# Where the first weight tiles of a fused retention and two-MLP kernel are loaded and converted

## The chip, the cores and the metric

The kernel runs on one core of a Trainium2 chip. The metric is device time in microseconds (us) for one launch. Times are medians of several runs; the profile is of one execution.

## The reference

Three layers follow one another, in float32. The first is linear attention with a decay per head ("retention") for 2 sequences of 768 positions, 8 heads of 64. Its output, 1536 tokens of 512 values, goes through a softplus MLP (512 to 2048 to 512) and then through an RMS-normalized SwiGLU MLP (512 to 1536 to 512).

```
state = gamma * state + k[t] outer v[t]          # per head, t = 0 .. 767
y[t]  = scale * q[t] @ state
x = y as (1536, 512)
x = softplus(x @ w_in) @ w_out
n = x / sqrt(mean(x * x) + 1e-6) * rms_g
out = (silu(n @ w_gate) * (n @ w_val)) @ w_out2
```

The weights of the MLPs arrive as 64-bit floats.

## The kernel before

**Tiles.** Tokens are handled in 12 chunks of 128 (6 for each sequence) and 4 blocks of 384 tokens (3 chunks each; `CB` is 3, `NB` is 4). A weight matrix is cut into tiles of 512 KB of doubles, 16 of `w_in` and 16 of `w_out`, used in groups of four: four of `w_in`, then four of `w_out`. Products are made in three terms of high and low parts, so that each value stands as two `fp32r` tiles.

**A chunk.** `load_next` starts the DMAs of q and k of one chunk and v of the chunk before it. `prep` scales v on POOL (GpSimd). `step_t` transposes k and q on PE (TensorE); ACT (ScalarE) copies k, DVE (VectorE) multiplies q by a table. `step_s` makes the scores on PE, and DVE multiplies them by two masks. `step_y` makes y on PE; ACT takes the high part of it and DVE the low part (`split`), and that is the x of the first MLP. `step_u` updates the state.

**A weight tile.** `load_weight` issues its DMA into one of three staging buffers (`STAGE`), if fewer than three tiles are loaded and not yet converted. `convert` turns the doubles into two float32 parts, in three pieces. The first is queued at once: two ACT reads of the staged tile (`c`, L166, and `a`, L167), two DVE operations (`w`, L168 and L170) and an add on POOL (L172). The second (`finish`: one DVE multiply, L181) and the third (`last`: the high part on ACT, L123, the low part on POOL, L124) are put on a list. `flush` runs what is on that list at that moment, and, if its argument is not false, calls `load_weight` as well. `weight` is what a product calls for its tile; where the tile isn't finished, it converts and flushes until it is:

```
while order[i] not in ready:
    if pos["conv"] <= i:
        assert convert()
    flush()
```

**The order of the work.** Everything is written out by hand: each engine works through its own queue in the order of the program. All loads but two stand on the queue of SP. An instruction that waits, a DMA issue too, holds what stands behind it on its queue. PSUM has eight banks that are taken in turn.

The front is the loop over `g` at L551. It takes chunks 0 to 2 to their x and prepares chunks 3 and 4. Behind it is the loop over weight groups `gr` and blocks `b`. In the first group the block that is multiplied is one ahead of the chunks still to be made: in each of four iterations `o`, `step_t` of a later chunk, the product `l1` of this block with one `w_in` tile (12 matmuls), then `step_y`, `step_u`, `step_s` of a chunk, and in block 0 one `convert` at the end. `l1`'s result goes through Abs, Exp and Ln on ACT (L358 to L360), a DVE operation (L361), and a split. In block 1, from the third iteration on, `l2` multiplies block 0's result by all four `w_out` tiles (12 matmuls for each of four outputs).

Of the kernel before, what the change touches and what calls it, by code (L numbers as in the profile page):

```python
# [27 lines left out]
def retention_softplus_swiglu(ctx: ExitStack, tc: tile.TileContext, q, k, v, w_in, w_out,  # L28
# [10 lines left out]
    CB = T // P  # L39
# [61 lines left out]
    def load_next(g, weight=False):  # L101
        if g + 1 < NCH:
            load(g + 1, 0)
            load(g + 1, 1)
        if weight:
            load_weight()
        if g < NCH:
            load(g, 2)
# [32 lines left out]
    def load_weight():  # L141
        i = pos["load"]
        if i >= len(order) or i >= pos["conv"] + STAGE:
            return False
        nm, f = order[i]
        t = stage_p.tile([P, N, 2], U32, tag="stage", name=f"st_{nm}{f}")
        src = srcs[nm]
        if nm in ("w_out", "w_out2"):
            nc.sync.dma_start(out=t, in_=src[f * P:(f + 1) * P])
        else:  # L150
            nc.sync.dma_start(out=t.rearrange("p (k f) two -> p k f two", k=KC),
                              in_=src[:, f * P:(f + 1) * P].rearrange("(k p) f two -> p k f two", p=P))
        staged[i] = t
        pos["load"] += 1
        return True

    def convert():
        i = pos["conv"]
        if i >= pos["load"] or not free:
            return False  # L160
        st = staged.pop(i)
        lo32, hi32 = st[:, :, 0], st[:, :, 1]
        c = cv_p.tile([P, N], U32, tag="c", name="c")
        a = cv_p.tile([P, N], F32, tag="a", name="a", bufs=3)
        w = cv_p.tile([P, N], U32, tag="w", name="w")
        nc.scalar.activation(out=c, in_=lo32, func=AF.Copy, scale=2.0 ** -29)  # L166
        nc.scalar.activation(out=a, in_=hi32.bitcast(F32), func=AF.Abs)  # L167
        nc.vector.tensor_scalar(out=w, in0=hi32, scalar1=3, scalar2=0x3FFFFFF8,  # L168
                                op0=ALU.logical_shift_left, op1=ALU.bitwise_and)
        nc.vector.scalar_tensor_tensor(out=w, in0=hi32, scalar=0xC0000000, in1=w,  # L170
                                       op0=ALU.bitwise_and, op1=ALU.bitwise_or)
        nc.gpsimd.tensor_tensor(out=c, in0=w, in1=c, op=ALU.add)  # L172
        slot[order[i]] = free.pop(0)
        t = ws_p.tile([P, 2, N], F32R, tag=f"ws{slot[order[i]]}", name=f"ws_{order[i][0]}")

        def last():
            split(t[:, 0], t[:, 1], a, nc.gpsimd)
            ready.add(order[i])

        def finish():  # L180
            nc.vector.scalar_tensor_tensor(out=a, in0=a, scalar=TINY, in1=c.bitcast(F32),  # L181
                                           op0=ALU.is_ge, op1=ALU.mult)
            deferred.append(last)


        deferred.append(finish if order[i][0] in ("w_in", "w_out") else lambda: deferred.append(finish))
        ws[order[i]] = t
        left[order[i]] = NB
        pos["conv"] += 1
        return True  # L190
# [12 lines left out]
    def flush(loads=True):  # L203
        todo = list(deferred)
        deferred.clear()
        for s in todo:
            s()
        if loads:
            load_weight()
# [39 lines left out]
    def prep(g):  # L249
        t = qkv[g][2]  # L250
        nc.gpsimd.tensor_tensor(out=t, in0=t, in1=dec[:, 1, 0, :, None].to_broadcast([P, H, D]), op=ALU.mult)
# [19 lines left out]
    def step_t(g, busy=0, order=(1, 0)):  # L271
        turn(g, busy, order)
        turned(g, order)

    def step_s(g):
        t = tr[g]
        sc = [bank("sc").rearrange("p (j t) -> p j t", j=NP) for _ in range(2)]
        for j in range(NP):
            for e in range(2):
                r = slice(e * D, (e + 1) * D)  # L280
                nc.tensor.matmul(sc[e][:, j, :], lhsT=t[r, 1, j, :], rhs=t[r, 0, j, :], start=True, stop=True)
        for e in range(2):
            nc.vector.tensor_tensor(out=t[:, 2 + e], in0=sc[e], in1=mask[e], op=ALU.mult)

    def step_u(g):
        c = g % CPB
        _, kk, vv = [qkv[g].pop(i) for i in range(3)]
        if c == CPB - 1:
            return
        u = bank("u")[:, 0:NP * D].rearrange("p (j t) -> p j t", j=NP)  # L290
        for j in range(NP):
            for e in range(2):
                h = 2 * j + e
                nc.tensor.matmul(u[e * D:(e + 1) * D, j, :], lhsT=kk[:, h, :], rhs=vv[:, NP * e + j, :],
                                 start=True, stop=True, skip_group_check=True)
        new, old = state[(c + 1) % 2], state[c % 2]
        if c == 0:
            nc.vector.tensor_copy(new, u)
        else:
            for j in range(NP):  # L300
                nc.vector.scalar_tensor_tensor(out=new[:, j], in0=old[:, j], scalar=step[:, j:j + 1], in1=u[:, j],
                                               op0=ALU.mult, op1=ALU.add)

    def step_y(g):
        c = g % CPB
        bi, ci = divmod(g, CB)
        if ci == 0:
            x[bi] = x_p.tile([P, 2, KC, T], F32R, tag="x", name=f"x{bi}")


        ys = [bank("y")[:, 0:2 * P].rearrange("p (i t) -> p i t", i=2) for _ in range(2)]
        t = tr.pop(g)

        if c:
            for i in range(2):
                for e, h in ((0, 0), (1, 1), (0, 1), (1, 0)):
                    nc.tensor.matmul(ys[e][h * D:(h + 1) * D, i, :], lhsT=state[c % 2][e * D:(e + 1) * D, 2 * i + h, :],
                                     rhs=t[e * D:(e + 1) * D, 0, 2 * i + h, :], start=(i == 0), stop=False,
                                     skip_group_check=True)
        for e in range(2):  # L320
            for i in range(2):
                for h in range(2):
                    j = 2 * i + h
                    nc.tensor.matmul(ys[e][h * D:(h + 1) * D, i, :], lhsT=qkv[g][2][:, NP * e + j, :], rhs=t[:, 2 + e, j, :],
                                     start=(c == 0 and i == 0), stop=True, skip_group_check=True)
        sl = slice(ci * P, (ci + 1) * P)
        for e in range(2):
            k2 = slice(2 * e, 2 * e + 2)
            split(x[bi][:, 0, k2, sl], x[bi][:, 1, k2, sl], ys[e])
# [220 lines left out]
    nc.scalar.activation(out=step, in_=tab[:, 0, :, 0], func=AF.Copy, scale=float(D) ** 0.5)  # L550
    for g in range(CB):  # L551
        load_next(g + 2)
        if g:
            load_weight()
        prep(g + 1)
        if g == CB - 1:
            nc.sync.dma_start(out=rg, in_=rms_g.rearrange("(k p) -> p k", p=P))
        step_y(g)
        step_u(g)
        step_s(g + 1)  # L560
        flush(False)
        if g < CB - 1:
            step_t(g + 2)
        flush(False)
        if 0 < g < CB - 1:
            convert()

    pend = None
    for gr in range(NG1):
        for b in range(NB):  # L570
# [6 lines left out]
            if gr == 0 and b < NB - 1:  # L577
                for o in range(G1):
                    g = (b + 1) * CB + o
# [95 lines left out]
```

## Time and profile before

| What | us |
|---|---|
| Median of 3 runs (lowest, highest) | 697.7 (696.85, 698.48) |
| The profiled execution | 698.23 |
| Its span in the profile | 696.5 |
| PE busy | 644.7 |
| DVE busy | 415.0 |
| ACT busy | 339.5 |
| POOL busy | 197.1 |

The span is from the first to the last instruction that the profiler saw; some 1.7 us of the execution lie around it. Busy shares are means over stages that differ: the first 140 us hold the attention and the first products, the rest is a dense succession of matmuls. L-numbers are lines of the kernel. "DMA share" is the mean busy share of 16 DMA engines.

### The profile page before, as it was taken

Reading aid. Unit: us, or ns where it says so; the run is one execution under the profiler, and the core shown is the slowest. Engines: PE = TensorE matmul, PEld = TensorE weight load, DVE = VectorE, ACT = ScalarE, POOL = GpSimd, SP = SyncE. Lnnn points to the kernel's source line nnn. Section 1 sums busy time; section 2 is a strip of 40 time slices with the busy share of each in tenths; the row PEclk is TensorE's granted clock in tenths of the full one; section 3 lists DMA queues with packets and bytes.
Section 4 is the critical chain, followed back from the end, with each engine's and each line's share of the span. In section 5 each row is a group of like instructions: output and inputs, shape, how many; then the busy total and the mean of one; then the engine's idle time right before and its main releaser. Section 6 shows DMA issues by size and latency. Waiting matters only on the chain.

```text
span 696.5 us, 10150 instructions
## 1 busy us (share of the span) xinstructions
PE 644.7 (93%) x3980; PEld 610.8 (88%) x3980; DVE 415.0 (60%) x713; ACT 339.5 (49%) x656; POOL 197.1 (28%) x156
## 2 busy tenths in 40 slices
PE   8656779999999999999999869999999999999997
PEld 7545668899999999999899759999999999999996
DVE  5643743545657574847657985586548773783432
ACT  3432723578767676759567543554225332441111
POOL 1322440336323241414101441263205330440000
PEclk9977979999999999999999989999999999999999
DMA  9945630223212120203001330132002220200112
GB/s 199 228 111 118 147 82 1 62 68 115 67 54 76 47 91 31 91 31 97 25 1 51 100 93 1 60 122 62 31 30 96 63 84 2 91 1 15 46 46 75
DMA packets 65567, 48.93 MB, mean 70 GB/s; under 512 B 39792, under 2 KB 60528, under 8 KB 65520
## 3 DMA queue, kind: packets, MB, share of 16 engines
q1 hardware_dynamic: 64320, 47.90, 24.5%
q8 instruction: 31, 0.51, 0.3%
q10 hardware_dynamic: 1200, 0.39, 0.2%
q14 instruction: 16, 0.13, 0.1%
HBM read 45.14 MB, written 3.15 MB: 69 GB/s over the span
## 4 chain that ended last, share of the span: by engine, by line
PE 60%; DVE 17%; ACT 13%; POOL 4%; issue 3%; SPq 2%; DMA 1%; POOLq 0%
PE h_w_val L341 12%; PE h_w_gate L341 11%; PE h L341 10%; PE l L495 9%; PE l L377 5%; PE acc L495 5%; PE acc L341 3%; POOL c L172 3%; DVE a L181 3%; DVE t L361 2%; ACT t L359 2%; PE acc L377 2%; ACT t L360 2%; DVE g L124 2%; DVE w L170 2%
## 5 line engine op out<-in xcount | busy, mean ns | idle before, releaser
L172 POOL TENSOR_TENSOR c<-w,c 128x512 uint32<-128x512 uint32 x68 | 89.0, 1308 | 335.1 <-DVE w L170 237.7
L341 PE MATMUL h<-x,ws_w_in 128*128 128x384 f32 x756 | 147.0, 343 | 13.4 <-ACT ws_w_in L123 13.0
L341 PEld LDWEIGHTS h<-x,ws_w_in 128*128 128x128 f32 x756 | 136.2, 194 | 14.4 <-ACT ws_w_in L123 13.7
L123 ACT ACTIVATE g<-t 128x384 fp32r<-128x384 f32 x112 | 58.7, 524 | 122.4 <-DVE t L476 84.2
L361 DVE SCALAR_TENSOR_TENSOR t<-h,t 128x384 f32<-128x384 f32 x63 | 35.1, 558 | 114.4 <-ACT t L360 114.4
L377 PE MATMUL l<-g,ws_w_out 128*128 128x384 f32 x516 | 97.4, 336 | 2.9 <-DVE g L124 1.4
L124 DVE TENSOR_TENSOR g<-t,g 128x384 fp32r<-128x384 f32 x112 | 75.2, 671 | 36.3 <-ACT g L123 35.3
L341 PE MATMUL h_w_val<-xn,ws_w_val 128*128 128x384 f32 x504 | 94.9, 336 | 0.0
L377 PEld LDWEIGHTS l<-g,ws_w_out 128*128 128x128 f32 x516 | 89.7, 188 | 4.5 <-DVE g L124 2.5
L341 PE MATMUL h_w_gate<-xn,ws_w_gate 128*128 128x384 f32 x492 | 92.7, 336 | 0.0
L341 PEld LDWEIGHTS h_w_val<-xn,ws_w_val 128*128 128x128 f32 x504 | 88.9, 188 | 2.3
L341 PEld LDWEIGHTS h_w_gate<-xn,ws_w_gate 128*128 128x128 f32 x492 | 87.0, 189 | 1.1
L495 PE MATMUL l<-ws_w_out,g 128*128 128x512 f32 x288 | 72.8, 396 | 3.8 <-ACT ws_w_out L123 2.8
L472 ACT ACTIVATE t<-t 128x384 f32<-128x384 f32 x48 | 25.2, 525 | 97.4 <-DVE t L471 97.4
L181 DVE SCALAR_TENSOR_TENSOR a<-a,c 128x512 f32<-128x512 f32 x68 | 62.7, 921 | 15.3 <-POOL c L172 15.2
L495 PEld LDWEIGHTS l<-ws_w_out,g 128*128 128x128 f32 x288 | 53.5, 188 | 14.4 <-ACT ws_w_out L123 3.3
L377 PE MATMUL acc<-g,ws_w_out 128*128 128x384 f32 x252 | 50.2, 348 | 5.0 <-ACT ws_w_out L123 4.2
L358 ACT ACTIVATE t<-h 128x384 f32<-128x384 f32 x63 | 30.4, 483 | 44.5 <-PE h L341 44.5
L476 DVE TENSOR_TENSOR t<-h_w_val,t 128x384 f32<-128x384 f32 x42 | 23.3, 554 | 47.6 <-PE h_w_val L341 46.4
L377 PEld LDWEIGHTS acc<-g,ws_w_out 128*128 128x128 f32 x252 | 45.8, 196 | 6.2 <-ACT ws_w_out L123 4.4
L124 POOL TENSOR_TENSOR ws_w_out<-a,ws_w_out 128x512 fp32r<-128x512 f32 x28 | 39.3, 1402 | 36.5 <-ACT ws_w_out L123 32.4
L495 PE MATMUL acc<-ws_w_out,g 128*128 128x512 f32 x144 | 35.4, 392 | 0.0
(122 smaller groups left out, 813.7 us busy)
## 6 DMA issues: line engine op xcount, KB each, us to landing
st_w_out<-in_moe_w_out_dram SPq DMA_DIRECT2D x28, 512.0 KB, 3.4
st_w_in<-in_moe_w_in_dram SPq DMA_DIRECT2D x16, 512.0 KB, 3.8
st_w_gate<-in_moe_w_gate_dram SPq DMA_DIRECT2D x12, 512.0 KB, 3.7
st_w_val<-in_moe_w_val_dram SPq DMA_DIRECT2D x12, 512.0 KB, 3.6
v<-in_v_dram SPq DMA_DIRECT2D x12, 256.0 KB, 4.6
q<-in_q_dram SPq DMA_DIRECT2D x23, 128.0 KB, 4.0
k<-in_k_dram SPq DMA_DIRECT2D x23, 128.0 KB, 4.0
out_dram<-o SPq DMA_DIRECT2D x11, 256.0 KB, 2.0
```

The source lines that it names most:

```text
L123: nc.scalar.activation(out=hi, in_=src, func=AF.Copy)
L124: eng.tensor_tensor(out=lo, in0=src, in1=hi.bitcast(F32), op=ALU.subtract)
L170: nc.vector.scalar_tensor_tensor(out=w, in0=hi32, scalar=0xC0000000, in1=w, op0=ALU.bitwise_and, op1=ALU.bitwise_or)
L172: nc.gpsimd.tensor_tensor(out=c, in0=w, in1=c, op=ALU.add)
L181: nc.vector.scalar_tensor_tensor(out=a, in0=a, scalar=TINY, in1=c.bitcast(F32), op0=ALU.is_ge, op1=ALU.mult)
L341: nc.tensor.matmul(h, lhsT=w[:, i, kk * P:(kk + 1) * P], rhs=src[:, j, kk, :], start=(n == 0), stop=(n == 3 * KC - 1))
L358: nc.scalar.activation(out=t, in_=h, func=AF.Abs)
L361: nc.vector.scalar_tensor_tensor(out=t, in0=h, scalar=0.0, in1=t, op0=ALU.max, op1=ALU.add)
L377: nc.tensor.matmul(p, lhsT=w[:, i, m * P:(m + 1) * P], rhs=g_t[b, f][:, j, :], start=(n == 0 and f == (0 if keep else fs[0])), stop=(n == ...
L472: nc.scalar.activation(out=t, in_=t, func=AF.Silu)
L476: nc.vector.tensor_tensor(out=t, in0=h, in1=t, op=ALU.mult)
L495: nc.tensor.matmul(p, lhsT=g_t[b, f][:, j, m * P:(m + 1) * P], rhs=w[:, i, :], start=(n == 0 and f == (0 if keep else grp[0])), stop=(n == ...
```

## The change

The front loads a weight tile with each of its three chunks, where it did so with the second and third only, and converts one tile in each of its three passes, where it did so in the second only. The rest of the code is the same; since conversions are counted, all later ones up to the fourth block stand elsewhere too.

```
     for g in range(CB):
         load_next(g + 2)
-        if g:
-            load_weight()
+        load_weight()
         prep(g + 1)
...
         flush(False)
         if g < CB - 1:
             step_t(g + 2)
         flush(False)
-        if 0 < g < CB - 1:
+        if True:
             convert()
```

On SP, in the front, from v of chunk 2 on; `st_` are weight tiles, and the names' numbers count allocations. Before:

```order
L81 DMA v_210<-in_v_dram 128x8x64
L84 DMA q_263<-in_q_dram 128x4x64 x2
L84 DMA k_266<-in_k_dram 128x4x64 x2
L81 DMA v_269<-in_v_dram 128x8x64
L151 DMA st_w_in_271<-in_moe_w_in_dram 128x4x256
L84 DMA q_343<-in_q_dram 128x4x64 x2
L84 DMA k_346<-in_k_dram 128x4x64 x2
L81 DMA v_349<-in_v_dram 128x8x64
L151 DMA st_w_in_351<-in_moe_w_in_dram 128x4x256
```

And now, the same stretch:

```order
L81 DMA v_210<-in_v_dram 128x8x64
L151 DMA st_w_in_212<-in_moe_w_in_dram 128x4x256
L84 DMA q_274<-in_q_dram 128x4x64 x2
L84 DMA k_277<-in_k_dram 128x4x64 x2
L81 DMA v_280<-in_v_dram 128x8x64
L151 DMA st_w_in_282<-in_moe_w_in_dram 128x4x256
L84 DMA q_357<-in_q_dram 128x4x64 x2
L84 DMA k_360<-in_k_dram 128x4x64 x2
L81 DMA v_363<-in_v_dram 128x8x64
L151 DMA st_w_in_365<-in_moe_w_in_dram 128x4x256
```

Every weight tile from the second on stands one chunk (q, k, v) further ahead.

On ACT, in the front, from the copy of chunk 2's k on; `x_` rows are the splits of a chunk's y, `c` and `a` the two reads of a staged weight tile, `ws_w_in` its high part. Before:

```order
L269 ACTIVATE at<-pt 128x512
L123 ACTIVATE x_213<-y 128x2x128
L123 ACTIVATE x_213<-acc_275 128x2x128
L269 ACTIVATE at<-acc_322 128x512
L166 ACTIVATE c<-st_w_in_172 128x512
L167 ACTIVATE a<-st_w_in_172 128x512
L123 ACTIVATE x_213<-acc_355 128x2x128
L123 ACTIVATE x_213<-y 128x2x128
L123 ACTIVATE ws_w_in<-a 128x512
L269 ACTIVATE at<-pt 128x512
L358 ACTIVATE t<-h 128x384
```

And now, up to the same split of chunk 2 and one row more:

```order
L269 ACTIVATE at<-pt 128x512
L166 ACTIVATE c<-st_w_in_172 128x512
L167 ACTIVATE a<-st_w_in_172 128x512
L123 ACTIVATE x_215<-y 128x2x128
L123 ACTIVATE x_215<-acc_286 128x2x128
L269 ACTIVATE at<-acc_334 128x512
L123 ACTIVATE ws_w_in<-a 128x512
L166 ACTIVATE c<-st_w_in_212 128x512
L167 ACTIVATE a<-st_w_in_212 128x512
L123 ACTIVATE x_215<-acc_369 128x2x128
L123 ACTIVATE x_215<-y 128x2x128
L123 ACTIVATE ws_w_in<-a 128x512
```

The first tile is read ahead of the split of chunk 1, the second ahead of that of chunk 2; behind these rows the third is read ahead of the first softplus (L358).

On DVE, in the third iteration of block 1, from a split to the next softplus; `w` are the rows of a conversion, here the tile that `l2` demands. Before:

```order
L124 TENSOR_TENSOR x_783<-acc_982,x_783 128x2x128
L301 SCALAR_TENSOR_TENSOR state_120<-state_119,step,u 128x64 x4
L283 TENSOR_TENSOR at<-sc,mask 128x512
L283 TENSOR_TENSOR at<-acc_1017,mask 128x512
L168 TENSOR_SCALAR w<-st_w_out_781 128x512
L170 SCALAR_TENSOR_TENSOR w<-st_w_out_781,w 128x512
L181 SCALAR_TENSOR_TENSOR a<-a,c 128x512
L361 SCALAR_TENSOR_TENSOR t<-h,t 128x384
```

And now:

```order
L124 TENSOR_TENSOR x_811<-acc_1010,x_811 128x2x128
L301 SCALAR_TENSOR_TENSOR state_120<-state_119,step,u 128x64 x4
L283 TENSOR_TENSOR at<-sc,mask 128x512
L283 TENSOR_TENSOR at<-acc_1045,mask 128x512
L361 SCALAR_TENSOR_TENSOR t<-h,t 128x384
```

The conversion of the fourth `w_out` tile is gone from here; it now stands in the first iteration of this block.

## Rows read from the trace of the kernel before

**Rows 1.** The page: busy tenths in 40 slices of 17.4 us, and PE's granted clock.

```profile
PE   8656779999999999999999869999999999999997
...
PEclk9977979999999999999999989999999999999999
```

**Rows 2.** Waits of PE over the span: us in total, times, longest.

```profile
PE h L341 <- ACT ws_w_in L123: 13.0, 3, 5.7
PE acc L341 <- ACT ws_w_in L123: 6.0, 1, 6.0
PE acc L377 <- ACT ws_w_out L123: 4.2, 1, 4.2
PE acc L262 <- DVE at L283: 3.6, 1, 3.6
```

**Rows 3.** Timeline of PE, first loop: start, duration, what [idle before, releaser].

```profile
25.50 2.38 PE L341 MATMUL h<-x,ws_w_in 128*128 128x384 f32 x12 [1.61 <-ACT ws_w_in L123]
...
31.48 0.60 PE L262 MATMUL acc<-ident,q 128*128 128x128 f32 x4
37.80 4.21 PE L341 MATMUL h<-x,ws_w_in 128*128 128x384 f32 x12 [5.71 <-ACT ws_w_in L123]
...
65.74 4.01 PE L341 MATMUL acc<-x,ws_w_in 128*128 128x384 f32 x12 [6.00 <-ACT ws_w_in L123]
69.59 2.27 PE L341 MATMUL h<-x,ws_w_in 128*128 128x384 f32 x12
```

**Rows 4.** Timeline of PE, the first products with `w_out`.

```profile
94.17 1.68 PE L377 MATMUL acc<-g,ws_w_out 128*128 128x384 f32 x8
...
100.97 1.01 PE L377 MATMUL acc<-g,ws_w_out 128*128 128x384 f32 x2 [4.19 <-ACT ws_w_out L123]
...
108.87 4.32 PE L377 MATMUL acc<-g,ws_w_out 128*128 128x384 f32 x24
```

**Rows 5.** Two windows: length, engines' busy us, then PEclk, DMA share, GB/s.

```profile
0.00:17.40 17.40, 14.87 (x176) 13.17 (x176) 9.86 (x22) 5.30 (x10) 3.22 (x10) 1.00 1.02 199
17.40:34.80 17.40, 11.92 (x164) 10.27 (x164) 11.18 (x27) 7.86 (x16) 5.68 (x5) 1.00 0.98 228
```

**Rows 6.** Timeline of SP's queue: when weight tiles one and three are issued.

```profile
8.95 1.11 SPq L151 DMA_DIRECT2D st_w_in<-in_moe_w_in_dram  x1
...
24.84 1.05 SPq L151 DMA_DIRECT2D st_w_in<-in_moe_w_in_dram  x1
```

**Rows 7.** DMA issues, 8.9 to 9.5 and 24.8 to 25.0: size, us to landing.

```profile
st_w_in<-in_moe_w_in_dram SPq DMA_DIRECT2D x1, 512.0 KB, 5.5
...
st_w_in<-in_moe_w_in_dram SPq DMA_DIRECT2D x1, 512.0 KB, 5.6
```

**Rows 8.** Timeline of POOL: the scaling of chunk 2's v.

```profile
19.12 1.04 POOL L251 TENSOR_TENSOR v<-v,dec 128x512 f32<-128x512 f32 x1 [5.43 <-DMA v<-in_v_dram]
```

**Rows 9.** Timeline of ACT in the front.

```profile
13.24 0.60 ACT L269 ACTIVATE at<-pt 128x512 f32<-128x512 f32 x1 [1.80 <-PE pt L262]
14.82 0.38 ACT L123 ACTIVATE x<-y 128x256 fp32r<-128x256 f32 x1 [0.98 <-PE y L324]
...
19.40 0.67 ACT L166 ACTIVATE c<-st_w_in 128x512 uint32<-128x512 uint32 x1
...
20.92 0.39 ACT L123 ACTIVATE x<-acc 128x256 fp32r<-128x256 f32 x1 [0.27 <-PE acc L324]
...
27.92 0.49 ACT L358 ACTIVATE t<-h 128x384 f32<-128x384 f32 x1 [1.99 <-PE h L341]
```

**Rows 10.** Timeline of DVE: a loop iteration's first and last, and conversion multiplies.

```profile
29.55 0.56 DVE L361 SCALAR_TENSOR_TENSOR t<-h,t 128x384 f32<-128x384 f32 x1 [4.17 <-ACT t L360]
...
34.87 0.68 DVE L264 TENSOR_TENSOR at<-acc,tab 128x512 f32<-128x512 f32 x1
36.39 0.69 DVE L181 SCALAR_TENSOR_TENSOR a<-a,c 128x512 f32<-128x512 f32 x1 [0.84 <-POOL c L172]
...
75.70 1.47 DVE L181 SCALAR_TENSOR_TENSOR a<-a,c 128x512 f32<-128x512 f32 x1
```

More of the change, by code (lines that the diff above doesn't have):

```diff
@@ L552, in retention_softplus_swiglu @@
         load_next(g + 2)
-        if g:
-            load_weight()
+        load_weight()
         prep(g + 1)
@@ L564, in retention_softplus_swiglu @@
         flush(False)
-        if 0 < g < CB - 1:
+        if True:
             convert()
```

## The prediction

> **What bounds the kernel now.** I read the slices first. PE (TensorE) is busy nine tenths or more of nearly every slice from about 105 us on; in front of that it is busy five to eight tenths, and the granted clock sags there too [rows 1]. So a change in the front pays in full if PE reaches its dense part earlier.
>
> Then the waits of PE: four stalls on ScalarE's weight tile `ws_w_in` (13.0 us in three, 6.0 us in one), one of 4.2 us on `ws_w_out`, and one of 3.6 us of transposes behind DVE's masks [rows 2]. PE's timeline places them. The first projection of the loop starts at 25.50, the second at 37.80 after 5.71 us idle, the fourth at 65.74 after 6.00 [rows 3]; the third waits much the same, for 13.0 less 5.7 leaves it up to 5.7. The code says why: one `convert()` stands at the end of each iteration, and the next `l1` demands that tile, so the whole chain of seven operations over ACT, DVE and POOL lies between two projections. The idle time costs clock as well: twelve matmuls take 2.38 us at 25.50 (2.4 GHz), 4.21 and 4.01 us after such a stall (1.2 GHz) [rows 3]. Later, two pieces of `l2` and a projection of 2.3 us lie between 94.17 and 108.87, with the 4.19 us stall among them: 14.7 - 2.3 = 12.4 us for a pair of `l2`; the pair at 108.87 takes 4.32 [rows 4].
>
> **The change, part by part.** The order of the instructions shows that it does what it says: three conversions stand in the front instead of one, the weight loads stand one chunk earlier on SP, and the conversion that `l2` demands in the second block is gone. No instruction is added or removed.
>
> *Transfers.* In the front the queue is saturated: 0.98 of the engines at 228 GB/s between 17.4 and 34.8 us [rows 5]. A weight tile of 0.524 MB is then worth 2.3 us, a chunk's q, k and v (0.786 MB) 3.45 us. The order is unchanged up to v of chunk 2, which is on the chip at 19.1 [rows 8]. Counting on from there in the new order, estimated landings are: second weight tile 21.4, q and k of chunk 4 23.7, v of chunk 3 24.8, third tile 27.1, q and k of chunk 5 29.4, v of chunk 4 30.6, fourth tile 32.9, q and k of chunk 6 35.2, v of chunk 5 36.3, two w_out tiles 38.6 and 40.9, q and k of chunk 7 43.2. A check: before, the third tile was issued at 24.84 and took 5.6 us [rows 6, 7], so 30.4; it now stands ahead of one chunk (3.45), which gives 27.0. SP waits for a free staging buffer from the fourth tile on, and the conversions that free them now come early.
>
> *Front, g = 0.* The first tile lands at 8.95 + 5.5 = 14.45 [rows 6, 7]. ACT comes to it after the copy at 13.24, waits 0.6 us and reads it twice, some 1.3 us (0.67 each [rows 9]). The split of chunk 1 behind it then begins at 15.8 instead of 14.82 [rows 9], 1 us late. I cost that at nothing: the y of chunk 2, next on PE, needs its scaled v, which POOL starts at 19.12 [rows 8]. Without that cover it would be 1 us.
>
> *g = 1.* ACT is ready for the second tile before it lands at 21.4, and reads it until 22.7; the split of chunk 2 behind it began at 20.92 [rows 9], so it is 1.8 us late, and DVE's work after it as much. PE is not held by that: the first `l1` has its weight, and starts when chunk 4 has been transposed, 23.7 + 1.1 = 24.8, against 25.50 [rows 3]. It ends at 27.1.
>
> *g = 2.* The third tile holds ACT until 27.1 + 1.3 = 28.4, the copy of k until 29.0; the first softplus takes 1.63 us from ACT's start to DVE's (27.92 to 29.55 [rows 9, 10]), so DVE begins at 30.6, 1.05 us later than now. That is the loss of the change.
>
> *Loop.* PE's own work for one iteration is 6.6 us (25.50 to 31.48 + 0.60 [rows 3]). DVE's train, from its first operation at 29.55 to the end of the last, 34.87 + 0.68, is 6.0 us; less 0.6 idle in it, plus the 0.69 of the conversion's multiply [rows 10], 6.1. When the multiply met work of POOL it took 1.47 instead of 0.69 [rows 10]: 6.9. I take 6.9 for an iteration; the bounds are PE's 6.6 and, if three DVE operations were held like this in each, 6.1 + 3 x 0.78 = 8.4. The transfers need 2.3 + 3.45 = 5.75 us, under all of these. Step by step: DVE starts at 30.6; its masks end 4.4 us later (6.1 less 1.7 for the three operations behind them), at 35.0, and the y of chunk 4 can go; that of chunk 5 goes one iteration later, 41.9. From there it is one round of PE, 6.6 us, to the first `l1` of the second block: 48.5. (In that round the transposes of chunk 7 are due at about 44.7; their data land at 43.2.) Before, that `l1` started at 69.59 [rows 3]: **21.1 us**.
>
> *Second block.* Its iterations stay as they are, the 3.6 us stall among them. At `l2` the last w_out tile has been converted an iteration earlier, so the 12.4 us become the 4.3 of the pair without a wait [rows 4]: **8.1 us**. The lower bound is 4.2, if the stall alone goes and the low clock stays.
>
> *Later.* From the fourth pass of the first weight group on the loads stand in the same order as before; nothing is gained or paid.
>
> **Sum.** 21.1 + 8.1 = 29.2 us, off a profiled execution of 698.2 (span 696.5), which lies 0.5 above the median of 697.7. So 697.7 - 29.2 = **668.5 us**.
>
> One rule speaks against this. The multiply at 75.70 took 1.47 us, with POOL at work beside it, and 0.69 at 36.39 [rows 10]. The Trainium skill, "SBUF — State Buffer", section "Who interferes with whom", says that a DVE instruction with both inputs in SBUF and a GpSimd instruction that reads SBUF want one port, which is an exclusive lock: the second waits until the first is done. By that rule the conversions, which so far ran while the rest stood still, would now hold DVE's operations of the loop more often. The trace agrees for the multiply; for the other two-input operations no row here shows it.
>
> **Rivals.**
> - *Transfers late.* For: the front's share of 0.98 [rows 5]. Against: in the loop 5.75 us of transfers meet 6.9 of work. At the 199 GB/s of the first stretch [rows 5] the 5.5 MB from 19.1 to chunk 7's data end at 46.7, not 43.2; its transposes wait 2 us, the conversions that hold ACT another 2: 672.5, and 676 if a pause of the queue comes on top. Chance 0.15.
> - *POOL and DVE hold one another*, as a mechanism of this kernel: 8.4 instead of 6.9 us in three iterations, and the same once in block two, 1.5 x 4 = 6: 674.5. For: the 1.47; against: other operations of the same train keep their length. Chance 0.15.
> - *The stall on w_out stays*, or a new one takes its place: 668.5 + 8.1 = 676.6. Against: its conversion stands an iteration earlier in the order. Chance 0.05.
> - *More is gained*: the 3.6 us stall of block two goes as well [rows 2]: 664.9, or 664 with the clock behind it. Chance 0.09.
> - *The change doesn't do what it says*: the tiles are ready no earlier, since their last steps wait for later flushes: 697.7. Against: in the order these steps stand ahead of the `l1` that reads them. Chance 0.02.
> - *Slower.* SP is one line, and each chunk now stands behind one more weight tile. An iteration needs 1.31 MB; three took 40.2 us before (65.74 less 25.50 [rows 3]). To lose the 8.1 us too they would have to take over 49, 16.4 each, which is a queue under 80 GB/s; at 75 it is 701. The row says 228. Chance 0.04.
>
> **Numbers.** The forecast has 0.50, its own width is 665.5 to 672. The range 663.5 to 679 adds the larger gain and the three cases of a smaller one, with their tails cut: about 0.88. Faster by over 0.2% (1.4 us, about what a measurement of this kernel can tell) 0.94; the same 0.02; slower 0.04.
>
> **What would show it.** PE's waits on `ws_w_in` fall from 19 us to under 2, the one on `ws_w_out` goes; the first four projections start 6.6 to 8 us apart and take 2.3 us each, at a full granted clock up to block two's stall; ACT waits about 1 us for the second weight tile; DVE's first operation of the loop's softplus starts near 30.6. The prediction is wrong if projections start 10 us or more apart with transposes waiting for data (transfers), if DVE's multiplies and subtractions take 1.4 us throughout (port), or if a new wait of PE stands at the pair of `l2`.

## The result, and the profile after

| What | before | after |
|---|---|---|
| Median (lowest, highest), us | 698.09 (696.85, 698.94) | 668.91 (668.46, 671.77) |
| Runs | 4 | 4 |
| The profiled execution, us | 698.23 | 668.47 |
| Its span, us | 696.5 | 666.8 |
| Mean granted clock | 0.971 | 0.989 |

The ratio is 0.9592, with an interval of 0.956 to 0.9623: 29.2 us less.

The slices of the page after the change, to be held against [rows 1]:

```profile
PE   8886989999999999999998699999999999999997
...
PEclk9998999999999999999998899999999999999999
```

The second to fourth tenths were 6, 5 and 6, and are 8, 8 and 6: PE reaches its dense part about two slices earlier. The clock sagged in the third, fourth and sixth slice; now it does so in the fourth alone. The dip in the middle is the norm between the two MLPs.

The waits of PE after the change (us in total, times, longest), which answer to [rows 2]:

```profile
PE acc L262 <- DVE at L283: 2.9, 1, 2.9
...
PE acc L317 <- DVE state L298: 2.6, 1, 2.6
...
PE h L341 <- DVE t L361: 0.5, 1, 0.5
```

No wait on `ws_w_in` is left (19 us before), and the 4.2 us of `l2` on `ws_w_out` is gone. In block two a wait for `state` has come, of 2.6 us; it was 0.5 before.

PE's timeline after the change (start, duration, what, idle time before and who ended it), which answers to [rows 3, 4]:

```profile
23.35 2.33 PE L341 MATMUL h<-x,ws_w_in 128*128 128x384 f32 x12
...
30.45 2.36 PE L341 MATMUL h<-x,ws_w_in 128*128 128x384 f32 x12
...
37.93 2.36 PE L341 MATMUL h<-x,ws_w_in 128*128 128x384 f32 x12
...
45.04 2.36 PE L341 MATMUL acc<-x,ws_w_in 128*128 128x384 f32 x12
47.24 2.24 PE L341 MATMUL h<-x,ws_w_in 128*128 128x384 f32 x12
...
58.57 0.32 PE L317 MATMUL acc<-at,state 64*64 64x128 f32 x1 [2.59 <-DVE state L298]
...
66.89 0.66 PE L262 MATMUL acc<-ident,q 128*128 128x128 f32 x4 [2.92 <-DVE at L283]
...
72.74 4.45 PE L377 MATMUL acc<-g,ws_w_out 128*128 128x384 f32 x24
77.03 2.24 PE L341 MATMUL h<-x,ws_w_in 128*128 128x384 f32 x12
```

The four projections of the first block stand 7.1, 7.5 and 7.1 us apart and none takes over 2.36 us, so all run at 2.4 GHz. The first `l1` of block two is at 47.24, where it was at 69.59 [rows 3]: 22.35 us are won by then. Between it and the first pair of `l2` lie 25.5 us (24.6 before, 69.59 to 94.17): 0.9 is lost. That pair takes 72.74 to 77.03, 4.3 us. The `l1` behind it was at 106.65 before, so 29.6 us are won here, all but 0.1 of what the spans differ by.

Three windows after the change (length, busy us of PE, PEld, DVE, ACT and POOL, then granted clock, DMA share, GB/s), to be held against [rows 5]:

```profile
0.00:17.40 17.40, 14.61 (x176) 12.98 (x176) 10.48 (x24) 6.37 (x12) 4.51 (x11) 1.00 1.11 215
17.40:34.80 17.40, 15.69 (x212) 13.76 (x214) 14.36 (x31) 10.93 (x23) 9.59 (x8) 1.00 0.96 225
...
52.20:69.60 17.40, 11.35 (x108) 9.74 (x106) 14.90 (x27) 9.28 (x20) 10.63 (x9) 0.90 1.00 208
```

The first window moves 215 GB/s where it moved 199, the second as much as before. PE's work in the second goes from 11.92 to 15.69 us, and DVE's and POOL's with it. In the last one, most of it block two, the clock's mean is 0.90: 1.7 us of full clock are missing, which is some 3.5 us at half clock, the only such stretch before 95 us. It lies behind the wait for `state`: the granted clock is 0.66 between 58 and 63 us, and 1.00 on both sides of that.

ACT in the front after the change, which answers to [rows 9]:

```profile
14.07 0.70 ACT L166 ACTIVATE c<-st_w_in 128x512 uint32<-128x512 uint32 x1 [0.45 <-DMA st_w_in<-in_moe_w_in_dram]
...
15.24 0.38 ACT L123 ACTIVATE x<-y 128x256 fp32r<-128x256 f32 x1
...
20.38 0.68 ACT L166 ACTIVATE c<-st_w_in 128x512 uint32<-128x512 uint32 x1 [0.72 <-DMA st_w_in<-in_moe_w_in_dram]
...
21.54 0.36 ACT L123 ACTIVATE x<-acc 128x256 fp32r<-128x256 f32 x1
...
26.03 0.63 ACT L123 ACTIVATE ws_w_in<-a 128x512 fp32r<-128x512 f32 x1 [3.86 <-DVE a L181]
26.57 0.68 ACT L166 ACTIVATE c<-st_w_in 128x512 uint32<-128x512 uint32 x1
```

The three weight tiles are read at 14.07, 20.38 and 26.57. For the first two ACT waits 0.45 and 0.72 us; the third lies there when ACT comes. What holds ACT ahead of the third is the second tile's multiply on DVE (3.86 us idle), which stands behind DVE's masks and starts at 24.66.

DVE after the change, which answers to [rows 10]:

```profile
24.66 1.33 DVE L181 SCALAR_TENSOR_TENSOR a<-a,c 128x512 f32<-128x512 f32 x1
...
29.84 0.56 DVE L361 SCALAR_TENSOR_TENSOR t<-h,t 128x384 f32<-128x384 f32 x1 [2.18 <-ACT t L360]
30.32 0.68 DVE L181 SCALAR_TENSOR_TENSOR a<-a,c 128x512 f32<-128x512 f32 x1
...
36.68 1.51 DVE L181 SCALAR_TENSOR_TENSOR a<-a,c 128x512 f32<-128x512 f32 x1 [0.38 <-POOL c L172]
...
43.80 1.51 DVE L181 SCALAR_TENSOR_TENSOR a<-a,c 128x512 f32<-128x512 f32 x1 [0.38 <-POOL c L172]
...
54.45 1.52 DVE L181 SCALAR_TENSOR_TENSOR a<-a,c 128x512 f32<-128x512 f32 x1 [0.89 <-POOL c L172]
55.89 1.63 DVE L124 TENSOR_TENSOR g<-t,g 128x384 fp32r<-128x384 f32 x1
```

And POOL at three of these moments:

```profile
24.40 1.05 POOL L251 TENSOR_TENSOR v<-v,dec 128x512 f32<-128x512 f32 x1 [0.86 <-DMA v<-in_v_dram]
...
36.61 1.04 POOL L251 TENSOR_TENSOR v<-v,dec 128x512 f32<-128x512 f32 x1
...
55.37 3.28 POOL L124 TENSOR_TENSOR ws_w_out<-a,ws_w_out 128x512 fp32r<-128x512 f32 x2
```

The conversion's multiply takes 0.68 us at 30.32, where POOL's scaling of v has 0.1 us left, and 1.51 where POOL began that scaling 0.07 us earlier: scaling ends at 37.65, and 37.65 + 0.69 is 38.3, close to the multiply's end at 38.19. At 55.89 the softplus's subtraction meets POOL's low part and takes 1.63 us instead of 0.55.

### The profile page after: what moved, and what is told of

Its sections match the earlier page's. It is cut to its first block, busy times and chain, and to the rows that moved or that the text cites. A ratio compares the mean times of both kernels' runs of the same rounds, so it can differ in the third digit from the quotient of the medians.

```text
span 666.8 us, 10151 instructions
## 1 busy us (share of the span) xinstructions
PE 635.6 (95%) x3980; PEld 603.6 (91%) x3980; DVE 417.9 (63%) x713; ACT 338.8 (51%) x656; POOL 197.3 (30%) x156
## 3 DMA queue, kind: packets, MB, share of 16 engines
q1 hardware_dynamic: 64320, 47.90, 25.1%
## 4 chain that ended last, share of the span: by engine, by line
PE 69%; DVE 15%; ACT 7%; POOL 3%; SPq 2%; issue 2%; DMA 2%; POOLq 0%; ACTq 0%
PE h_w_val L341 13%; PE h L341 12%; PE h_w_gate L341 12%; PE l L495 10%; PE l L377 8%; PE acc L495 5%; PE acc L377 4%; DVE a L181 3%; PE acc L341 3%; POOL c L172 3%; DVE g L124 2%; DVE w L168 2%; DVE w L170 2%; SPq L84 1%; DVE t L361 1%
## 5 line engine op out<-in xcount | busy, mean ns | idle before, releaser
L341 PE MATMUL h<-x,ws_w_in 128*128 128x384 f32 x756 | 143.6, 338 | 0.5 <-DVE t L361 0.5
L341 PEld LDWEIGHTS h<-x,ws_w_in 128*128 128x128 f32 x756 | 132.8, 189 | 1.0 <-DVE t L361 0.8
L361 DVE SCALAR_TENSOR_TENSOR t<-h,t 128x384 f32<-128x384 f32 x63 | 35.1, 557 | 94.2 <-ACT t L360 94.2
L181 DVE SCALAR_TENSOR_TENSOR a<-a,c 128x512 f32<-128x512 f32 x68 | 65.0, 956 | 13.4 <-POOL c L172 13.3
L358 ACT ACTIVATE t<-h 128x384 f32<-128x384 f32 x63 | 30.5, 483 | 32.9 <-PE h L341 32.9
L377 PE MATMUL acc<-g,ws_w_out 128*128 128x384 f32 x252 | 47.0, 335 | 0.0
L377 PEld LDWEIGHTS acc<-g,ws_w_out 128*128 128x128 f32 x252 | 43.9, 188 | 0.1
```

The costliest lines, as they stand in the source:

```text
L341: nc.tensor.matmul(h, lhsT=w[:, i, kk * P:(kk + 1) * P], rhs=src[:, j, kk, :], start=(n == 0), stop=(n == 3 * KC - 1))
L358: nc.scalar.activation(out=t, in_=h, func=AF.Abs)
L361: nc.vector.scalar_tensor_tensor(out=t, in0=h, scalar=0.0, in1=t, op0=ALU.max, op1=ALU.add)
L377: nc.tensor.matmul(p, lhsT=w[:, i, m * P:(m + 1) * P], rhs=g_t[b, f][:, j, :], start=(n == 0 and f == (0 if keep else fs[0])), stop=(n == ...
```

## The experiments

Theory: PE waited in the front for the chain of a conversion, so what counts is that a conversion stands at least one projection ahead of the `l1` that demands it; the loads only have to keep up; and `l2` gains its 8.1 us because the last `w_out` tile is converted an iteration earlier. Rivals: the earlier loads did it; the gain is one of `w_out`'s place alone; DVE and POOL holding one another eats a part. Each kernel's diff is against the changed kernel unless the text says otherwise. Ratios are to the kernel before on the same chip.

### The loads alone

```diff
-        if True:
+        if 0 < g < CB - 1:
             convert()
```

> Only the earlier loads; one conversion in the front, as before. My theory (PE waits for the chain of a conversion, not for the tile's transfer) expects no gain: 697 to 699 us, four waits on ws_w_in of 5 to 6 us each but the first, and the stall on the last w_out tile of some 4 us as before. The rival that the earlier transfer brings the gain expects 670 to 685. A third, that pushing the chunks back by 2.3 us costs something, expects 700 or a little over.

Measured: 698.32 us, ratio 1.0015 (1.0005 to 1.0024). PE's waits in this kernel:

```profile
PE h L341 <- ACT ws_w_in L123: 12.0, 3, 5.7
PE acc L341 <- ACT ws_w_in L123: 5.5, 1, 5.5
```

The earlier loads alone win nothing: 17.5 us of waits where 19.0 were. (The 1 us that it is slower is not in the front: at the end of the first pair of `l2` it is 0.4 ahead. A projection of the third block took 3.85 us instead of 2.38; see the last section.)

### The conversions alone

```diff
-        load_weight()
+        if g:
+            load_weight()
```

> Conversions in all three passes, but the loads where they were before: tiles two and three are read in the same pass that loads them. They land at about 24.5 and 30.4 instead of 20.4 and below 26.6, and ACT and DVE stand before them with the chunk's split and the first softplus behind: the first softplus on DVE begins near 34 instead of 29.8, the rest of the loop is the same: 673 us (671.5 to 674.5). The rival that loads don't matter expects 669; the rival that transfers bring most of the gain expects over 680.

Measured: 672.35 us, 0.9641 (0.9625 to 0.9657). ACT in this kernel, and then PE:

```profile
24.54 0.67 ACT L166 ACTIVATE c<-st_w_in 128x512 uint32<-128x512 uint32 x1 [4.49 <-DMA st_w_in<-in_moe_w_in_dram]
```

```profile
26.10 3.87 PE L341 MATMUL h<-x,ws_w_in 128*128 128x384 f32 x12 [2.08 <-ACT x L123]
```

ACT stands 4.49 us at a tile that has not landed, with the split of chunk 2 behind it; the first `l1` waits 2.08 us for that x and runs for the most part at half clock. The change's 0.72 has become 4.49, and the change is some 3.4 us better (0.9592 against 0.9641 of 698). In the front the extra load is worth more: the first pair of `l2` ends at 82.39 here and at 77.03 in the change, 5.4 us apart. Some 1.5 of them go again far behind, at a projection of the third block that takes 3.83 us in the change and 2.38 here (last section). The conversions are worth the rest.

### Two conversions in the front instead of three

```diff
-        if True:
+        if g:
             convert()
```

> Loads as in the change, but conversions in the second and third pass of the front only: two ahead instead of three. My theory in its sharper form says that a conversion needs one whole iteration of lead and no more: no wait of PE on ws_w_in above 1 us, at most 1 us on the last w_out tile, 667 to 670, level with the change's 668.9. The rival that each conversion taken into the front saves one stall expects half of the gain to go, 678 to 684.

Measured: 670.14 us, 0.9611 (0.9591 to 0.9631), 0.1 above the expected range and not told from the change by the intervals. PE and DVE of this kernel:

```profile
25.34 2.68 PE L341 MATMUL h<-x,ws_w_in 128*128 128x384 f32 x12 [1.61 <-ACT ws_w_in L123]
...
45.92 2.36 PE L341 MATMUL acc<-x,ws_w_in 128*128 128x384 f32 x12 [0.77 <-ACT ws_w_in L123]
```

```profile
24.54 1.30 DVE L168 TENSOR_SCALAR w<-st_w_in 128x512 uint32<-128x512 uint32 x1
...
25.87 1.66 DVE L170 SCALAR_TENSOR_TENSOR w<-st_w_in,w 128x512 uint32<-128x512 uint32 x1
```

The first `l1` waits 1.61 us as before, above the 1 us expected, since its tile is still converted in the last pass but one; behind it at most 0.77. One projection of lead is nearly all that is needed, and the third conversion buys a little slack and the 1.6 us: the first pair of `l2` ends at 78.65, 1.6 behind the change. (The third block's projection, 2.35 us here and 3.83 in the change, gives most of that back.) The two DVE rows (0.42 and 0.69 where POOL is idle) stand beside POOL's scaling and low part.

### The `w_out` term by itself: the kernel before with one conversion more

Diff against the kernel before; the front stays as it was.

```diff
                     if b == 0 or o < 2:
                         convert()
+                    if b == 1 and o == 0:
+                        convert()
```

> The kernel before with one conversion more in the first iteration of block 1 and nothing else: the front and block 0 are untouched. The term of 8.1 us for the pair of l2 should show by itself, less 1 to 2 us for the crowded iteration: 689.5 to 692, with no PE wait on ws_w_out. If that stall was only covered time, 696 to 698.

Measured: 693.6 us, 0.9944 (0.9929 to 0.9959), a miss by 1.6 us on the upper side. PE and DVE of this kernel:

```profile
83.40 0.55 PE L281 MATMUL sc<-at 64*128 64x128 f32 x1 [2.64 <-DVE at L264]
...
98.87 4.45 PE L377 MATMUL acc<-g,ws_w_out 128*128 128x384 f32 x24
103.16 2.24 PE L341 MATMUL h<-x,ws_w_in 128*128 128x384 f32 x12
```

```profile
83.64 2.42 DVE L181 SCALAR_TENSOR_TENSOR a<-a,c 128x512 f32<-128x512 f32 x2
85.99 1.63 DVE L124 TENSOR_TENSOR g<-t,g 128x384 fp32r<-128x384 f32 x1
```

The pair takes 4.3 us: the term of 8.1 is there. But it starts at 98.87 where it started at 94.17, 4.7 later, with two conversions in one iteration. Block two up to the pair takes 29.5 us instead of 24.6. Of these 4.9, DVE's crowding makes 3.5: PE waits 2.64 us for the scores' operand, which waited 0.6 there before, and the transposes behind DVE's masks come another 1.5 later (90.30). The projection behind them adds 0.9, at 4.19 us where 3.29 was: from 83.4 to the pair the granted clock is 0.58 here, and 0.86 over the same work before (81.6 to 94.2). 8.1 less 4.7 is 3.4, and 3.5 is what the ends of the pairs differ by (106.65 to 103.16). The size that the expectation missed is the crowding, with the clock behind it.

### The opposite: the change without block two's own conversions, the early `w_out` one among them

```diff
-                    if b == 0 or o < 2:
+                    if b == 0 or (b == 2 and o < 2):
                         convert()
```

> The change without the two conversions in block 1, so that l2 demands the last w_out tile again as in the kernel before. By the sum the 8.1 us come back, less 1 to 2 us that the emptier iterations of block 1 give: 674.5 to 677.5, with a PE wait of some 4 us on ws_w_out. If the gain lay in the front alone, 667 to 669.

Measured: 674.63 us, 0.9666 (0.9649 to 0.9684). PE's longest wait in this kernel:

```profile
PE acc L377 <- ACT ws_w_out L123: 5.0, 1, 5.0
```

The pair takes from 71.13 to 83.61, 12.5 us, 8.2 more than in the change. Block two ahead of it takes 23.5 us (47.59 to 71.13) instead of 25.5, and the wait of 2.9 us at L262 falls to 0.8. So the term is 8.2, and the two conversions that are left out, the one that pays it and the next, cost 2.0 of block two's time. The wait for `state` stays (2.57): it isn't theirs.

### Where block two's 0.9 us goes: POOL's scaling behind the conversion

In the block loop `prep` of the next chunk is moved behind the second `flush`, so that POOL takes the low part first.

```diff
                         load_next(g + 2)
-                        prep(g + 1)
                     after()
...
                         flush()
+                        if g + 1 < NCH:
+                            prep(g + 1)
```

> The change, with POOL's scaling of the next v behind the last steps of a conversion in the loop instead of ahead of them. If the port which POOL and DVE share sets the loop's pace, the multiply at L181 is back at 0.69 us instead of 1.51 and each iteration is some 0.8 us shorter: 664 to 666.5. If PE sets the pace, or another DVE operation is held in its place, 668 to 670.

Measured: 665.83 us, 0.9544 (0.953 to 0.9559). DVE and PE of this kernel:

```profile
37.28 0.69 DVE L181 SCALAR_TENSOR_TENSOR a<-a,c 128x512 f32<-128x512 f32 x1 [0.39 <-POOL c L172]
```

```profile
57.45 0.32 PE L317 MATMUL acc<-at,state 64*64 64x128 f32 x1 [1.77 <-DVE state L298]
```

The multiply is back at 0.69 us in the loop (in block two one meets the low part and takes 1.76), and the wait for `state` is 1.8. The time is the expected one, its reason only in part: the loop itself wins 0.2 us and not 0.8 an iteration (first `l1` of block two at 47.04), since the y now waits up to 0.98 for its v; block two takes 24.1 us (to 71.11) instead of 25.5. These rows make 1.6 us, and the two profiled spans differ by 1.7 (666.8 and 665.1); the medians differ by 3.1.

### One conversion less in the first block's last iteration

```diff
-                    if b == 0 or o < 2:
+                    if o < (CB if b == 0 else 2):
                         convert()
```

> The change without the conversion in the fourth iteration of block 0, so that each later one is an iteration later. My reading of the change's trace is that the wait of PE for the state in block 1 (2.6 us) comes from two conversions close together on DVE and POOL: it should fall to under 1 us, the clock stay full there, and the last w_out tile still be ready in time or within 1 us: 665.5 to 667.5. If that wait comes from the order of the chunk's own work, 668.5 to 670; if the last w_out tile is late, 670 to 674 with a PE wait on it.

Measured: 667.2 us, 0.9562 (0.9545 to 0.9578). PE in this kernel:

```profile
63.62 1.11 PE L262 MATMUL acc<-ident,q 128*128 128x128 f32 x4 [3.62 <-DVE at L283]
64.38 4.19 PE L341 MATMUL h<-x,ws_w_in 128*128 128x384 f32 x12
```

The conversion that stood at 51.84, 3.7 us behind the one before it, is gone, and so is the wait for `state`. Yet the wait at L262 grows to 3.6 and the `l1` behind it runs at half clock, which the expectation did not have: block two takes 25.1 us, and the ratio is not told from the change's. So the wait for `state` needs the crowding; by the time, moving it alone is inconclusive.

### Both

> The change with both remedies: POOL's scaling of v behind the conversion's last steps in the loop, and no conversion in the chunkless fourth iteration of block 0. If both savings are real and separate, 663 to 665.5. If they are the same saving (the multiply held by POOL in the first iterations of block 1), no better than the better one alone, 665.5 to 667.

The kernel has the two edits above. Measured: 664.37 us, 0.9519 (0.9501 to 0.9538), whose interval lies under the change's: the lowest time here, faster than the kernels before and after. Its interval overlaps that of the scaling moved alone (0.953 to 0.9559); in the rows it is ahead of that by 2.1 us at the end of the first pair of `l2` (73.33 against 75.40). PE in it:

```profile
68.80 4.69 PE L377 MATMUL acc<-g,ws_w_out 128*128 128x384 f32 x24
```

The first `l1` of block two is at 46.08, 1.2 us earlier than in the change, and block two takes 22.7 us. No wait for `state` is left.

### Holding, or POOL's order

Moving the scaling also changed POOL's order. Here the scaling of v is left out in the block loop and the order kept: `prep(g + 1)` is deleted there.

> The changed kernel with POOL's scaling of v left out of the block loop (the chunks from 5 on stay unscaled, so this part of the computation is missing; POOL is free of 1.0 to 1.25 us in each iteration). In e4_prep_late the scaling was moved behind DVE's step on the low part, that step fell from 1.51 to 0.69 us and the state wait from 2.6 to 1.8 us, but POOL's order on its queue was changed with it. If the two engines holding one another is what cost block two its 0.9 us: the step takes 0.69 us here too, the wait for state is under 2 us, no matmul waits for a late v, and the time is 664 to 666 us. If it was POOL's order (the low part taken earlier) and not the holding: the step on the low part may be short, but the state wait stays at 2.5 to 2.9 us and the time is 667.5 to 669 us.

Measured: 665.48 us, 0.9535 (0.9519 to 0.9552). DVE and PE of this kernel:

```profile
36.40 0.69 DVE L181 SCALAR_TENSOR_TENSOR a<-a,c 128x512 f32<-128x512 f32 x1 [0.38 <-POOL c L172]
```

```profile
55.81 0.32 PE L317 MATMUL acc<-at,state 64*64 64x128 f32 x1 [1.06 <-DVE state L298]
```

The multiply takes 0.69 in the loop, the wait for `state` is 1.1, the first `l1` of block two stands at 46.14 and the pair at 70.67: 24.5 us, about what it was before the change. (A projection at the low clock is in it, 3.57 us at 63.70, where the change has 2.33 and the kernel before had 3.29.) So the 0.9 us goes with POOL's scaling beside the conversion, and not with the order of the two; this kernel and the one with the scaling moved agree within their intervals. The rows carry this and not the time: the third block's projection takes 2.37 us here and 3.83 in the change, so some 1.5 us of the gain on the change are the clock's. How much of the 0.9 is the held DVE and how much POOL's own microsecond, by which its low parts are later, the two kernels don't separate: in block two one multiply here still meets the low part and takes 1.76 us.

## Why the prediction was right, and where it was off

| Step | predicted | measured |
|---|---|---|
| Split of chunk 1 on ACT | 15.8 | 15.24 |
| ACT reads the second tile | 21.4 | 20.38 |
| First `l1` | 24.8 | 23.35 |
| DVE's first softplus operation | 30.6 | 29.84 |
| y of chunk 4 to y of chunk 5 | 35.0 to 41.9 | 33.73 to 40.84 |
| First `l1` of block two | 48.5 | 47.24 |
| Won up to there | 21.1 | 22.35 |
| Block two up to the pair | 0 | -0.9 |
| Pair of `l2` | 8.1 | 8.2 |
| Sum | 29.2 | 29.6 |

**What held.** The mechanism: PE waited for a conversion between two projections, and with the conversions ahead it does not. The loads alone win nothing, the conversions alone all but 3.4 us of the time (5.4 in the front's rows). The `w_out` term was sized right, 8.2 by the change and by the kernel that takes it out again. The iteration of 6.9 us, DVE's train with one held multiply, was 7.1 (33.73 to 40.84): the train without a hold takes 5.9 where 6.1 was counted (29.84 to 35.76), the hold 0.82 where 0.78 was taken, and ahead of the multiply DVE waits 0.38 us for POOL's add, which was counted at nothing.

**What was luck.** The sum is 0.4 us off what the rows give, because 1.25 us more in the front and 0.9 us less in block two set one another off. The terms that were off follow.

**The transfers were some 1 us earlier than counted.** ACT reads the second tile at 20.38, where 21.4 was counted. The count put that tile wholly behind v of chunk 2, at the mean of 228 GB/s. But the queue was not full ahead of that: between 16.5 and 18 us it moved 17 to 124 GB/s in the kernel before, and 253 to 342 now. And a weight tile passes faster than the mean: 331 GB/s between 17 and 18 us, where most of what moves is the tile, against 224 between 18.8 and 20.4, where q, k and v move. The kernel with `w_out` late has the same front, finds the hole again (67 to 133 GB/s), and still reads its tile at 20.11, with 362 GB/s between 18 and 19 us; so 2.3 us for a tile was too much even without the hole. The first `l1`, 1.45 us early, does not wait for data at all: from the y of chunk 2 at 19.92 on PE works without a listed wait, and the transposes of chunk 4 find their data at 22.50. The rival of late transfers fell with it.

**"The loss of the change"**, 1.05 us at the third tile, was 0.3 (29.84 against 29.55). The front's g = 2 step named the wrong thing too: ACT did not wait for the third tile but, 3.86 us, for the second tile's multiply on DVE, which took 1.33 beside POOL's scaling at 24.40.

**The mis-sized term is block two.** "Its iterations stay as they are" was wrong by 0.9 us. Two conversions stand 3.7 us apart on DVE there (48.17 and 51.84) and a third at 59.63, each with POOL's operations; the multiply at 54.45 and the subtraction at 55.89 were each held, so the state was copied late (wait 2.6 instead of 0.5) and the clock fell behind that. The 0.9 is a net: 2.2 us are lost by the time `state` is read (58.57 less 47.24, against 78.69 less 69.59), and 1.3 come back behind it, for the later stall went from 3.6 to 2.9 and the projection there takes 2.33 us instead of 3.29. Without POOL's scaling beside it block two takes 24.5 us, with the scaling behind the conversion 24.1. Both causes make the wait for `state`: it is gone with one conversion less, and down to 1.1 without the scaling.

**The rival of POOL and DVE holding one another** was the right place at about a sixth of its price of 6 us. The Trainium skill, "SBUF — State Buffer", section "Who interferes with whom", says that the port which a DVE instruction with two SBUF inputs shares with GpSimd is an exclusive lock. The trace agrees, with 1.51 against 0.69 at the multiply, and with 1.63 against 0.55 at a subtraction. No row of the prediction shows the latter, but the kernel before has it farther back: a subtraction at 417.20 takes 1.64 us. But in the loop one operation an iteration met POOL, which the 6.9 held already, and not three.

**Later** was put at nothing, and is that in sum, though by two differences of the clock, far behind the change, that cancel one another (last section).

## What to carry to other kernels

Where each engine works through one queue in the order written, a conversion needs to stand about one whole consumer ahead, as here, and the first one ahead of the loop; a load that comes early without that changes nothing, and a conversion ahead of its load turns into a wait of everything queued behind it. Cost such a move twice: once for the stall it removes, once for the iteration into which it goes, where two conversions more, or two close together, cost 2 to 5 us here, the clock's part with it. When DVE and POOL both gain work in a stretch, see which of their operations begin within a microsecond of one another, and move POOL's deferrable one.

## What was not expected of the hardware

A DVE operation that reads one tensor, the uint32 step at L168, was also held beside POOL: 1.30 us against 0.42 (the rows of the kernel with two conversions). The kernel before has this too, farther back: 1.47 us at 216.39, 0.12 behind the start of a low part. POOL's own operations are held when they begin second: a low part takes 1.28 us alone, 1.48 in the kernel with two conversions, and 1.84 at 149.49 in the kernel before, 0.01 behind the start of a DVE operation that keeps its 0.69.

The clock falls or does not fall at the same place of the same work. Far behind the change, a projection of the third block ran at half clock in the changed kernel. The row of it there, and of before:

```profile
99.28 3.83 PE L341 MATMUL h<-x,ws_w_in 128*128 128x384 f32 x12
```

```profile
129.04 2.38 PE L341 MATMUL h<-x,ws_w_in 128*128 128x384 f32 x12
```

It was slow with the loads alone (3.85), with the scaling moved (3.92) and with both edits (3.80), and not in the other six (2.35 to 2.38). So of the 29.6 us, 28.3 were left behind it (132.97 to 104.70, the next pair of `l2`). The other 1.3 came back at the norm between the MLPs, where the clock fell less. The same 70 us, 28.27 apart, in the kernel before and after:

```profile
343.27:413.27 70.00, 60.19 (x321) 57.31 (x320) 52.53 (x108) 41.74 (x82) 17.47 (x13) 0.93 0.17 53
```

```profile
315.00:385.00 70.00, 60.11 (x325) 57.33 (x324) 52.93 (x108) 41.82 (x82) 17.57 (x13) 0.95 0.16 53
```

0.02 of 70 us is 1.4. What decides such a fall was not tried; it means that differences of 1 to 1.5 us between two of these kernels can be the clock's alone, and only rows tell.
